# Turning the row maxima with one matmul and one DMA per group, a new order of SyncE's DMAs, maxima 17 units ahead, and six early output tiles

## The chip, the cores and the metric

One of the eight NeuronCores of a Trainium2 chip runs the whole kernel. The metric is device time in microseconds of one execution. Five engines work beside each other, each with its own instruction queue in program order: TensorE (PE) multiplies, VectorE (DVE), ScalarE (ACT) and GpSimd (POOL) compute element by element, and SyncE (SP) only issues DMAs. An instruction that waits for a semaphore holds everything behind it on its own engine. Nearly all DMAs of the first half of this kernel are issued by SP.

## The reference

Causal attention with a multiplicative decay, on 8 batches of 8 heads, 576 tokens and head dimension 64, and after it a mixture of experts, which picks one of 8 experts for each token.

```python
scores = scale * np.matmul(q, k.transpose(0, 1, 3, 2))
cum = np.cumsum(np.log(np.clip(f, 0.0001, 1.0)), axis=-1)
decay = cum[:, :, :, None] - cum[:, :, None, :]
scores = np.where(causal, -1000000000.0, scores + decay)
scores = scores - np.max(scores, axis=-1, keepdims=True)
attn = np.exp(scores); attn = attn / (np.sum(attn, axis=-1, keepdims=True) + 1e-09)
x = np.matmul(attn, v)                       # heads side by side: (8, 576, 512)
# per token: e = argmax(x @ w_gate), or the expert of the token before where a local gate says so
out[b, s] = p[e] * (np.maximum(x[b, s] @ w1[e], 0.0) @ w2[e])
```

## The kernel before

**Attention in 25 units.** Every batch is cut into 25 units of work in five groups. A group 0 to 3 is a pair of heads with five units (`cunit`, `aunit` twice, `bunit`, `cunit`); group 4 has the last 64 queries of all heads, in four `d1unit` and one `d2unit`. A unit has stages, each on one engine: `sc` (PE: scores, transposed, keys on the partitions), `ex` (ACT: exp), `hi` (ACT: the f16 upper part of the result, tile `ph`), `lo` (DVE: the rest, tile `pl`) or, for the units in `SUBS`, `sub` (PE subtracts `ph`) and `lo2` (ACT copies the rest), `av` (PE: three products with the parts of v), and for some `n1` and `n2` (DVE: division by the sum).

**The maxima.** Exp needs the maximum of each query row, which is taken ahead. For each unit there is a maximum: `sm` (PE: leading scores, queries on the partitions, into tile `sm` of the two-bank pool `psM`) and `mx` (DVE: negated row maximum into a column of `nmq`). When the last maximum of a group is there, `sh` follows: DVE transposes `nmq` in blocks of 32 x 32 into `nmt` (line 918), and SP sends it with four DMAs, one per block row, into row 70 of the group's part of `QB` (line 927). Row 70 meets a row of ones in `KB`, so the second matmul of each score block (line 872, `KB` and `QB`, 71 rows) subtracts the maximum. Thus the scores of a group wait for `mx`, the transpose, the place of the four DMAs in SP's queue, and their landing. `LM` (10) says how many units ahead of its own unit a maximum is put into the planner's lines.

**Turned q and k.** The leading scores and the scores need q and k of the next batch turned: SP loads them as f32, POOL splits them into f16 parts (`t16q`, `t16k`), PE transposes eight blocks (`tq`, line 397), ACT or DVE evicts them into `Aq`, `Ak` (`eq`, line 406 to 410; `TE` says which engine), and SP copies the upper part into `QB`, `KB` (line 377, 381). `TS` lists from which unit of the batch before a group's turn may start, `LI` the units at which the loads of the batch after are issued. The maxima of a group need the copies of that group.

**x.** The normalised output `xn` is split by POOL (`xr`, `xl`), turned by a DMA transpose on SP (line 741, 772: `xt`, `xlt`) and written to DRAM (line 747, 779: `xs`) for the experts.

**The planner.** The order of instructions on each engine is made while the program is built. `issue` keeps a line per stage and a `clock` per engine, works out the earliest start of each line's head (`start_of`) from costs written beside each stage, adds a lead per stage (`LEADS`) and emits the stage that is earliest. POOL's work is emitted in portions (`pump`, line 342) with a clock of its own: `clock["POOL"] = max(clock["POOL"], clock["PE"]) + 1.1 * c` (line 348). The planner has no clock for SP: each DMA stands in SP's queue where the code that issues it happens to run, the transposes of x right behind the emission of POOL's split, v's loads with `ship` at given units. For the maxima and the turned copies it counts 3500 ns from the end of the producer to the landing (line 1179).

**The early experts.** While the routing of the last batches is worked out, PE runs the first three tiles of 128 tokens of experts 0 and 1. Their six outputs are evicted by ACT into tiles `o` (line 1763) of which there are three, scaled by POOL (line 1734) when the probabilities are there, and scattered by an indirect DMA (line 1735); a tile is free when its scatter has landed.

Of the kernel before, what the change touches and what calls it, by code (L numbers as in the profile page):

```python
# [34 lines left out]
SUBS = ((2, 4, 10, 13, 14),) * 8  # L35
# [15 lines left out]
LI = (12, 14)  # L51
PX = 5
XI = 2
# [6 lines left out]
RANKS = ((134.0, 26.4, 114.9, 242.4, 23.9, 178.9, 202.3, -22.5, 146.6, -22.2, -144.4, -13.8, 9.1, 28.6, 47.5, 5.3),) * 8  # L60
LEADS = ((-214, -102, -294, -258, -210, -30, -680, -129, -443, -278, -132, -206, -132, -210, -43),) * 8
LM = 10
DMAW = 0.0
# [16 lines left out]
XL = 5300  # L80
# [17 lines left out]
def kernel(  # L98
# [291 lines left out]
    def group(b, nm, j):  # L390
        U = {}

        def tq():
            t16 = Tq[b][nm + "t"]
            U["pt"] = psS.tile([128, 8, 128], F16, name="st")
            for a in range(4 if j == 4 else 8):
                nc.tensor.transpose(U["pt"][:, a], t16[:, 8 * j + a], ident16)

        def eq():
            A, pt = Tq[b][nm + "A"], U["pt"]  # L400
            dst, src = flat(A[:, 8 * j:min(8 * j + 8, 36)]), flat(pt[:, 0:4 if j == 4 else 8])
# [9 lines left out]
            if j < 4:  # L411
                copy_hi(b, nm, 2 * j, 2 * j + 2)
            else:
                copy_last(b, nm)

        c = 0.5 if j == 4 else 1.0
        eng, cost = ("ACT", 130 + 880 * c) if TE[b][nm][j] == "A" else ("DVE", 100 + 570 * c)
        return {"key": (b, nm, j), "tq": ("PE", 460 * c, tq, {"psS": 1}, {}), "eq": (eng, cost, eq, {}, {"psS": 1})}

    def prep_turned(b, nm):  # L420

        def begin():
            add_turns(99)
            if line["eq"]:
                issue((line["eq"][-1][0], "eq"))
            new_prep(b, nm)
            prep_aug(b, nm)

        def half(g0, g1):
            R = {}  # L430

            def parts(i):
                t, t16 = LT[b, nm], Tq[b][nm + "t"]
# [12 lines left out]
    def prep_v(b):  # L446
        i = b % 2

        def part(g0, j):
            return hi_lo(VH[i][:, g0:g0 + 16, 0:64], VL[i][:, g0:g0 + 16, 0:64], LT[b, "v"][:, g0:g0 + 16], 8)[j][1]()  # L450

        def rest(u):
            split(vlast(VH[i], u)[:, :, 0:64], vlast(VL[i], u)[:, :, 0:64], LT[b, "v"][u * 64:(u + 1) * 64, 32:36], False)

        return ([(1024, lambda g0=g0, j=j: part(g0, j)) for g0 in (0, 16) for j in range(3)] +
                [(768, lambda u=u: rest(u)) for u in range(2)])

    def prep(b):

        q, k, v = prep_turned(b, "q"), prep_turned(b, "k"), prep_v(b)  # L460
        done = set()

        def mark(nm):
            return (0, lambda: done.add(nm))

        bulk.extendleft(reversed([(c, lambda: True, lambda c=c: load_v(b, last=c == 4, cs=range(c, min(c + 1, 4))))
                                  for c in range(5)]))
        last = [(5500, init_route)] if b == 2 else []
        if b + 1 < B:
            for nm, i in ("q", LI[0]), ("k", LI[1]):  # L470
                bulk.append((i, lambda nm=nm: nm in done, lambda nm=nm: (new_load(b + 1, nm), load_main(b + 1, nm, 0, 0, H))))
                bulk.append((i + 1, lambda nm=nm: nm in done, lambda nm=nm: load_main(b + 1, nm, 1, 0, H)))
                bulk.append((i + 2, lambda nm=nm: nm in done, lambda nm=nm: load_last(b + 1, nm)))
        return q[:1] + k[:1] + q[1:5] + k[1:5] + q[5:] + [mark("q")] + k[5:] + [mark("k")] + v + last
# [205 lines left out]

    HS = {}
# [10 lines left out]
    def due_head(nm):  # L692
        head_hi(HS[2, nm], 2, nm)
        head_b(HS[2, nm], 2, nm)
        head_lo(HS[2, nm], 2, nm)
        turned[0, nm, -2] = clock["ACT"] + 960 - 3500
        clock["ACT"] += 960
        clock["DVE"] = max(clock["DVE"] + 640, clock["ACT"] + 800)

    def head_3(nm):  # L700
# [6 lines left out]
        def eq():  # L707
            for f in head_hi, head_b, head_lo:
                f(U["st"], 3, nm)
            clock["DVE"] = max(clock["DVE"], clock["ACT"] + 1100) + 640  # L710

        return {"key": (0, nm, -1), "tq": ("PE", 500, tq, {"psS": 1}, {}), "eq": ("ACT", 960, eq, {}, {"psS": 1})}
# [19 lines left out]
    def finish_main(b, xn):  # L732
        xr = pools["small"].tile([128, 4, 2, DM], F16, name="xr", bufs=1)
# [11 lines left out]

        def put_x(r):
# [4 lines left out]
        bulk.extendleft([(0 if b == B - 1 else PX + 2 * r, lambda: 2 in R, lambda r=r: put_x(r)) for r in (1, 0)])  # L751
# [8 lines left out]
        for c in range(0, 4, 2):  # L760
            todo += hi_lo(xr[:, c:c + 2, 0, :], xr[:, c:c + 2, 1, :], xm[:, c:c + 2], 1)
            todo.append((0, lambda c=c: turn_x(c)))
        queue.extendleft(reversed(todo))

    def finish_last(b, xnl):
        xl = pools["small"].tile([128, 2, 4, 64], F16, name="xl", bufs=1)
# [4 lines left out]
        def turn_x():  # L771
# [3 lines left out]
            XR[b] = max(clock["POOL"], clock["PE"]) + XL  # L775
# [10 lines left out]
        else:  # L786
            for i, x in enumerate(hi_lo(xl[:, 0], xl[:, 1], xnl, 4) + [(0, turn_x)]):
                queue.insert(min(XI, len(queue)) + i, x)

# [36 lines left out]
    nmq = cst.tile([128, 2, 5, 32], F16, name="nmq")  # L826
    nmt = cst.tile([128, 2, 5, 32], F16, name="nmt")
    nc.gpsimd.memset(nmq, 0.0)

    def compute(b, T):  # L830
# [69 lines left out]
        def maximum(g, scoref, maxf, cost, takes=1, last=None):  # L900
# [6 lines left out]
            if last:  # L907
                M["sh"], M["key"] = ("DVE", cost[2], last, {}, {}), (b, "shift", g)
# [7 lines left out]
        def turn_shift(g):  # L916

            nc.vector.transpose(nt[:, g], nq[:, g])
            f = flat(QBb[70:71])
            for i in range(4):  # L920
                src = nt[32 * i:32 * i + 8, g]
                if g < 4:
                    dst = f[:, 1024 * g:1024 * g + 1024].rearrange("p (y i x) -> p y i x", i=4, x=32)[:, :, i]
                else:
                    src = src[0:4]
                    dst = f[:, 4096 + 256 * (i // 2):4352 + 256 * (i // 2)].rearrange("p (y i x) -> p y i x", i=2, x=32)[:, :, i % 2]
                nc.sync.dma_start(out=dst, in_=src)
# [56 lines left out]
        def d1unit(j):  # L984
# [14 lines left out]

            def sh():  # L1000
                nc.vector.tensor_tensor(nq[:, 4, 0:4], nm[:, 0:4], nm[:, 4:8], ALU.min)
                turn_shift(4)
# [11 lines left out]
            maximum(4, sm, mx, (680 if j == 0 else 300, 930 if j == 0 else 598, 250), 1 + (j == 0), sh if j == 3 else None)  # L1014
# [72 lines left out]
        def cunit(j, r):  # L1087
# [20 lines left out]
            maximum(j, sm, mx, (275, 598, 160), 1, (lambda: turn_shift(j)) if r == 1 else None)  # L1108
# [42 lines left out]
    STAGES = ("sm", "mx", "mn", "sh", "sc", "ex", "hi", "lo", "sub", "lo2", "av", "n1", "n2", "tq", "eq")  # L1151
# [3 lines left out]
    clock = {"PE": T0, "ACT": T0 + 900, "DVE": T0 + 1300, "POOL": T0}  # L1155
    due = deque()
    pools = {}
# [5 lines left out]
    def start_of(st):  # L1163
# [78 lines left out]
    def issue(until=None):  # L1242
        while any(line.values()):
# [5 lines left out]
            ready = [x for x in ready if x[0] is not None]  # L1249
            if not ready:  # L1250
# [11 lines left out]
            for r, c in takes.items():  # L1262
                for _ in range(c):
                    room[r].remove(min(room[r]))
            fn()
            clock[eng] = t + cost
            ends[n, st] = t + cost, eng
            if st in ("eq", "sh"):
                turned[u["key"]] = t + cost + (0 if st == "eq" else DMAW)
# [468 lines left out]
    def experts(W, xT, nt, prob, scat, hp, op, width=608, every=6, half=None, sums=None):  # L1738
# [276 lines left out]
    issue()  # L2015
    late = early_weights(stage, W0, range(6, 8), shared=7)
    queue.extend(late[:-4])
    pump(0)
    ship(99)
    while chain:  # L2020
# [150 lines left out]
    def close_attention():  # L2171
# [6 lines left out]
        EX["oe"] = ectx.enter_context(tc.tile_pool(name="oe", bufs=3))  # L2178
# [466 lines left out]
```

## Time and profile before

| | us |
|---|---|
| median of 3 runs (lowest, highest) | 915.76 (915.65, 917.53) |
| the profiled execution | 924.86 |
| its span, first to last instruction | 923.1 |
| PE busy in the span | 769.3 (83%) |
| DVE, ACT, POOL busy | 544.4, 476.2, 442.5 |
| attention, about | 31 to 515 |
| experts, about | 515 to 923 |

The profile is of one execution and is a little longer than the median. A busy time is the union of the engine's instructions; a wait is the idle time just ahead of an instruction, put down to what ended it. The granted clock is the share of TensorE's full clock that was granted in a stretch: 1.00 is 2.4 GHz and 0.50 is 1.2 GHz.

### The profile page before, as it was taken

To read this page: it belongs to the slowest core of one execution; us is meant where nothing else is said; L and a number is where in the kernel's file an instruction comes from. 1 tells how busy PE (TensorE), PEld (TensorE's weight loads), DVE (VectorE), ACT (ScalarE), POOL (GpSimd) and SP (SyncE) were. 2 spreads that over 40 slices of the span, in tenths; PEclk is the share of its full clock that TensorE was granted. 3 is DMA by queue.
4 is the path that set the end of the run, shared out by engine and by line. 5 is a ranking of instruction groups with operands and counts; after the bars stand their busy time and mean duration, and the time that the engine had idled before them with its cause. 6 is when DMAs were issued, how large, how long until landed. Compare 5 with 4: busy or idle time off the path is not lost. (4 is left out here: it accounts for less than half of the span.)

```text
span 923.1 us, 24010 instructions
## 1 busy us (share of the span) xinstructions
PE 769.3 (83%) x9730; PEld 579.2 (63%) x9730; DVE 544.4 (59%) x1263; ACT 476.2 (52%) x837; POOL 442.5 (48%) x498
## 2 busy tenths in 40 slices
PE   6639678578685886868956999999999999998996
PEld 3528567568575775857855645656756566657484
DVE  8528446548585695765854477442666766565740
ACT  8529546567575584766843342332545353534441
POOL 5882671835469256693355623233521181247201
PEclk9769868879798897888976999999999999999999
DMA  5633753573747537573277647365653838181501
GB/s 146 153 68 89 163 125 85 125 165 70 152 106 137 147 70 138 133 137 67 55 202 160 188 153 228 90 152 189 136 209 88 236 89 254 56 264 51 109 14 43
DMA packets 192812, 120.96 MB, mean 131 GB/s; under 512 B 131374, under 2 KB 167662, under 8 KB 192658
## 3 DMA queue, kind: packets, MB, share of 16 engines
q1 hardware_dynamic: 186620, 100.28, 45.8%
q0 software_dynamic: 6080, 19.13, 6.6%
q8 instruction: 77, 1.26, 0.6%
q14 instruction: 35, 0.29, 0.1%
HBM read 72.25 MB, written 19.32 MB: 99 GB/s over the span
## 5 line engine op out<-in xcount | busy, mean ns | idle before, releaser
L872 PE MATMUL st<-QB,KB 71*128 71x128 f16 (+2 forms) x960 | 132.5, 229 | 99.2 <-DMA QB<-nmt 98.7
L938 ACT ACTIVATE st<-st 128x512 f32<-128x512 f32 (+1 forms) x200 | 116.3, 582 | 103.4 <-PE st L878 79.6
L872 PEld LDWEIGHTS <-KB 71*128 71x128 f16 (+1 forms) x960 | 94.1, 109 | 108.3 <-issue 60.6
L946 DVE TENSOR_TENSOR pl<-st,ph 128x512 f16<-128x512 f32 (+1 forms) x160 | 105.1, 665 | 66.2 <-ACT ph L942 54.7
L882 DVE TENSOR_REDUCE nmq<-sm 128x1 f16<-128x512 f32 (+3 forms) x224 | 110.8, 531 | 52.2 <-PE sm L878 49.8
L942 ACT CAST ph<-st 128x512 f16<-128x512 f32 (+1 forms) x200 | 115.0, 578 | 46.6 <-PE xp L896 41.0
L872 PE MATMUL st<-Aq,Ak 128*128 128x128 f16 (+2 forms) x960 | 133.8, 229 | 3.9 <-DVE pl L946 3.7
L1779 PE MATMUL z<-xT,wh 128*128 128x384 f16 (+5 forms) x640 | 120.6, 299 | 5.2 <-DVE hl L1756 5.2
L1768 POOL DMA_INDIRECT out_dram<-o,ranki x26 | 36.4, 1400 | 159.1 <-ACT o L1766 79.8
L896 PE MATMUL xp<-VH,pl 128*128 128x65 f16 (+1 forms) x960 | 98.6, 201 | 1.8 <-DVE pl L946 1.7
L1821 PE MATMUL y<-ul,hh 128*128 128x512 f16 x264 | 100.1, 379 | 0.0
L1821 PE MATMUL y<-uh,hl 128*128 128x512 f16 x264 | 100.1, 379 | 0.0
L1821 PE MATMUL y<-uh,hh 128*128 128x512 f16 x264 | 100.1, 379 | 0.0
L896 PE MATMUL xp<-VH,ph 128*128 128x65 f16 (+1 forms) x960 | 99.1, 202 | 0.0
L863 PE MATMUL sm<-KB,QB 70*128 70x256 f16 (+4 forms) x448 | 81.1, 306 | 21.4 <-DMA KB<-Ak 17.6
L896 PE MATMUL xp<-VL,ph 128*128 128x65 f16 (+1 forms) x960 | 98.7, 201 | 0.0
L872 PEld LDWEIGHTS <-Ak 128*128 128x128 f16 (+1 forms) x960 | 93.8, 109 | 7.2 <-issue 3.9
L896 PEld LDWEIGHTS <-ph 128*128 128x128 f16 (+1 forms) x1920 | 90.1, 107 | 7.6 <-issue 3.7
L1821 PEld LDWEIGHTS <-hh 128*128 128x128 f16 x528 | 51.3, 98 | 57.5
L896 PEld LDWEIGHTS <-pl 128*128 128x128 f16 (+1 forms) x960 | 80.1, 107 | 2.2 <-DVE pl L946 2.0
L1779 PEld LDWEIGHTS <-wh 128*128 128x128 f16 x640 | 63.3, 100 | 28.6 <-issue 6.8
L1779 PE MATMUL z<-xT,wl 128*128 128x384 f16 (+5 forms) x320 | 79.8, 299 | 0.0
(450 smaller groups left out, 1747.5 us busy)
## 6 DMA issues: line engine op xcount, KB each, us to landing
stg<-in_moe_w_dram SPq DMA_DIRECT2D x64, 512.0 KB
xs<-xr SPq DMA_DIRECT2D x16, 512.0 KB
ldq<-in_q_dram SPq DMA_DIRECT2D x14, 512.0 KB
ldk<-in_k_dram SPq DMA_DIRECT2D x14, 512.0 KB
ldv<-in_v_dram SPq DMA_DIRECT2D x56, 128.0 KB
QB<-Aq SPq DMA_DIRECT2D x30, 128.0 KB
KB<-Ak SPq DMA_DIRECT2D x30, 128.0 KB
QB<-nmt SPq DMA_DIRECT2D x128, 0.5 KB
```

The lines of the kernel that those rows point to most:

```text
L863: nc.tensor.matmul(st[p0:p0 + m, co:co + n], lhsT=block(QBb, 70, h, c), rhs=rhs, start=(first and co == col), stop=True, skip_group_check= ...
L872: nc.tensor.matmul(st[p0:p0 + m, col:col + n], lhsT=block(tk, kk, h, kc), rhs=block(tq, kk, h, c), start=(ps == 0 and (i == 0 or p0 > 0 an ...
L882: nc.vector.tensor_reduce(dst, src, axis=AX.X, op=ALU.max, negate=True)
L896: nc.tensor.matmul(xo, lhsT=a[:, c0:c0 + m], rhs=w[:, vi, :], start=False, stop=(i == n - 1 and jj == 2), skip_group_check=True)
L938: nc.scalar.activation(U["st"][:, :cols], U["st"][:, :cols], AF.Exp)
L942: nc.scalar.copy(U["ph"][:, :cols], U["st"][:, :cols])
L946: nc.vector.tensor_tensor(U["pl"][:, :cols], U["st"][:, :cols], U["ph"][:, :cols], ALU.subtract)
L1768: nc.gpsimd.indirect_dma_start(out=outf, out_offset=bass.IndirectOffsetOnAxis(ap=scat(t)[0:m], axis=0), in_=o[0:m], in_offset=None, bounds ...
L1779: nc.tensor.matmul(z[:, a, 0:wd], lhsT=w[:, d, fc * 128:(fc + 1) * 128], rhs=xT[:, x, a * wd:(a + 1) * wd], start=(i == 0), stop=(i == len ...
L1821: nc.tensor.matmul(y[0:m], lhsT=a[:, fc, t * 128:t * 128 + m], rhs=u[:, fc], start=(i == 0), stop=(i == len(prods) - 1))
```

## The change

- `nmq` shrinks to 8 columns per group and `nmt` becomes 8 rows of 128. Instead of `sh` on DVE there are two stages: `sh` on PE, a matmul of `nmq` (as weights, 8 or 4 columns) with the identity into the bank of the group's last maximum, and `se`, a copy out of PSUM (DVE by `SE`). That bank is freed by `se`, not by `mx`. One DMA sends 8 x 128 values; group 4 has two. The minimum of group 4 (line 1001) moves into `mx`.
- A DMA may be posted with the time at which the planner thinks its producer ends and a cost on SP. `deliver` emits the earliest one and moves a new `clock["SP"]`; `issue` delivers a posted DMA before it emits any stage that starts later. Posted are the sends of maxima, the copies into `QB` and `KB`, the decay rows, the loads of q, k and v, the transposes and writes of x. A consumer calls `need`, so that a tile's load is emitted before POOL's work on it.
- What counts as landed is `clock["SP"] + LAND` (2000 ns), not the producer's end plus 3500 ns.
- `LM` is 17; the parameters of the planner (`RANKS`, `LEADS`, `SW`, `TS`, `TE`, `LI`, `PX`, `XI`) are other ones; `SUBS` has six units instead of five.
- The early experts have six tiles `o`.

```diff
-SUBS = ((2, 4, 10, 13, 14),) * 8
+SUBS = ((1, 7, 12, 20, 21, 24),) * 8
-LI = (12, 14)
-PX = 5
-XI = 2
+LI = (11, 9)
+PX = 6172
+XI = 9
-SW = ((-271, 0, 0),) * 8
-TS = ({'q': (4, 15, 19, 21, 24), 'k': (10, 13, 20, 24, 24)},) * 8
-TE = ({'q': 'AAAAA', 'k': 'DAAAA'},) * 8
+SW = ((-969, 0, 0),) * 8
+TS = ({'q': (4, 16, 18, 21, 19), 'k': (10, 15, 17, 21, 22)},) * 8
+TE = ({'q': 'AADDA', 'k': 'AAAAA'},) * 8
...
-LM = 10
-DMAW = 0.0
+LM = 17
+LAND = 2000.0
+SE = ('DVE', 160)
...
+    def post(ready, cost, fn, tag=None):
+        heapq.heappush(mail, (ready, sent[0], cost, fn, tag))
+        sent[0] += 1
+        if "run" not in EX:
+            deliver()
+
+    def deliver():
+        ready, _, cost, fn, _ = heapq.heappop(mail)
+        clock["SP"] = max(clock["SP"], ready) + cost
+        fn()
+
+    def need(tag):
+        while any(x[4] == tag for x in mail):
+            deliver()
...
+        def posted_x(c):
+            post(clock["POOL"], 2600, lambda: turn_x(c), ("x", b))
+            for r in range(2 if c else 0):
+                post(clock["POOL"] + PX * (r + 1), 630, lambda r=r: put_x(r), ("x", b))
...
-    nmq = cst.tile([128, 2, 5, 32], F16, name="nmq")
-    nmt = cst.tile([128, 2, 5, 32], F16, name="nmt")
-    nc.gpsimd.memset(nmq, 0.0)
+    nmq = cst.tile([128, 2, 5, 8], F16, name="nmq")
+    nmt = cst.tile([8, 2, 5, 128], F16, name="nmt")
...
-                M["sh"], M["key"] = ("DVE", cost[2], last, {}, {}), (b, "shift", g)
+                M["mx"] = "DVE", cost[1], maxf, {}, {"psM": takes - 1}
+                M["sh"] = "PE", 80, lambda: turn_shift(g, last()), {}, {}
+                M["se"] = SE[0], SE[1], lambda: put_shift(g, last()), {}, {"psM": 1}
...
-        def turn_shift(g):
-
-            nc.vector.transpose(nt[:, g], nq[:, g])
+        def turn_shift(g, st):
+
+            m = 8 if g < 4 else 4
+            nc.tensor.matmul(st[0:m, 0:128], lhsT=nq[:, g, 0:m], rhs=ident16, start=True, stop=True, skip_group_check=True)
+
+        def put_shift(g, st):
+            m = 8 if g < 4 else 4
...
+                nc.vector.tensor_copy(nt[0:m, g], st[0:m, 0:128])
             f = flat(QBb[70:71])
-            for i in range(4):
-                src = nt[32 * i:32 * i + 8, g]
...
-                nc.sync.dma_start(out=dst, in_=src)
+
+            def send():
+                if g < 4:
+                    nc.sync.dma_start(out=f[:, 1024 * g:1024 * g + 1024], in_=nt[0:8, g])
...
+                turned[b, "shift", g] = clock["SP"] + LAND
+
+            post(clock[SE[0]], 600 if g < 4 else 1200, send)
...
-                after.append((turned[key] + 3500, "POOL"))
+                after.append((turned[key], "POOL"))
...
+            if mail and mail[0][0] <= min((x[0] for x in ready), default=1e9):
+                deliver()
+                continue
...
-            o = (EX["oe"] if op is ep else op).tile([128, DM], F32, name="o", bufs=3)
+            o = (EX["oe"] if op is ep else op).tile([128, DM], F32, name="o", bufs=6 if op is ep else 3)
```

## Rows read from the trace of the kernel before

**Rows 1.** The page's 40 slices: TensorE's granted clock, in tenths.
```profile
PEclk9769868879798897888976999999999999999999
```

**Rows 2.** Windows: stretch, length, busy PE, PEld, DVE, ACT, POOL; clock, DMA.
```profile
63.00:124.40 61.40, 46.33 (x819) 40.53 (x820) 32.82 (x75) 37.48 (x64) 35.91 (x39) 0.81 0.52 110
...
sum 411.90, PE 316.05 PEld 279.77 DVE 262.90 ACT 263.02 POOL 226.80; mean PE 45.15 PEld 39.97 DVE 37.56 ACT 37.57 POOL 32.40
```

**Rows 3.** Windows between the long waits, the same seven batches.
```profile
302.90:350.30 47.40, 43.91 (x881) 39.10 (x881) 39.46 (x102) 36.28 (x66) 21.29 (x26) 0.95 0.50 116
...
sum 347.90, PE 314.40 PEld 279.19 DVE 242.67 ACT 255.55 POOL 180.54; mean PE 44.91 PEld 39.88 DVE 34.67 ACT 36.51 POOL 25.79
```

**Rows 4.** Waits of PE, 20 to 520 us: total, times, longest.
```profile
PE st L872 <- DMA QB<-nmt: 98.7, 18, 15.9
PE sm L863 <- DMA KB<-Ak: 17.6, 5, 4.9
```

**Rows 5.** Timeline of DVE near 287 us: start, length, instruction.
```profile
286.69 0.21 DVE L918 STREAM_TRANSPOSE nmt<-nmq 128x32 f16<-128x32 f16 x1
```

**Rows 6.** Timeline of SP's queue, 282 to 305 us.
```profile
283.96 1.57 SPq L741 DMA_TRANSPOSE xt<-xr  x1
285.64 1.92 SPq L772 DMA_TRANSPOSE xlt<-xl  x1
...
288.95 1.82 SPq L741 DMA_TRANSPOSE xt<-xr  x1
...
294.44 4.36 SPq L203 DMA_DIRECT2D ldv<-in_v_dram  x2
298.90 2.82 SPq L927 DMA_DIRECT2D QB<-nmt  x4
```

**Rows 7.** Timeline of PE; in brackets the idle time before and what ended it.
```profile
31.61 0.27 PE L872 MATMUL st<-QB,KB 71*128 71x128 f16 x1 [6.02 <-DMA QB<-nmt]
...
302.88 0.27 PE L872 MATMUL st<-QB,KB 71*128 71x128 f16 x1 [11.37 <-DMA QB<-nmt]
302.94 0.31 PE L872 MATMUL st<-Aq,Ak 128*128 128x128 f16 x1
```

**Rows 8.** Windows behind nine of the waits; columns as in rows 2.
```profile
302.90:307.80 4.90, 4.90 (x65) 4.90 (x66) 2.37 (x6) 2.15 (x4) 1.92 (x2) 0.50 0.77 169
...
sum 47.80, PE 47.75 PEld 43.13 DVE 13.67 ACT 21.47 POOL 22.81; mean PE 5.31 PEld 4.79 DVE 1.52 ACT 2.39 POOL 2.53
```

**Rows 9.** Groups by shape, 20:520 us: count, busy us, mean ns, idle.
```profile
L949 PE MATMUL st<-ph,minus 128*128 128x512 f16 x40 | 17.0, 425 | 0.8 <-ACT ph L942 0.7
...
L946 DVE TENSOR_TENSOR pl<-st,ph 128x512 f16<-128x512 f32 x152 | 101.8, 679 | 65.4 <-ACT ph L942 54.1 <-PE xp L896 7.9 <-PE st L949 3.1
...
L918 DVE STREAM_TRANSPOSE nmt<-nmq 128x32 f16<-128x32 f16 x40 | 8.4, 209 | 1.0
...
L819 DVE TENSOR_TENSOR L<-st,half 128x36 f32<-128x36 f32 x7 | 1.3, 190 | 0.1
...
L406 ACT ACTIVATE Aq<-st 128x1024 f16<-128x1024 f16 x30 | 30.7, 1026 | 17.0 <-PE st L397 16.9
...
L954 ACT CAST pl<-st 128x512 f16<-128x512 f32 x40 | 23.4, 588 | 11.2 <-PE st L949 11.0
```

**Rows 10.** Waits of ACT from 515 us on: total, times, longest.
```profile
ACT o L1763 <- DMA out_dram<-o,xs: 14.9, 3, 6.8
```

**Rows 11.** Timeline of PE at the early experts.
```profile
586.62 0.27 PE L1779 MATMUL z<-xT,wh 128*128 128x256 f16 x1 [2.17 <-DVE hl L1756]
```

**Rows 12.** The window behind it; columns as in rows 2.
```profile
586.70:592.00 5.30, 5.30 (x35) 4.11 (x35) 1.65 (x9) 0.77 (x2) 2.72 (x4) 0.68 0.26 99
```

**Rows 13.** Two dense windows of 20 us; columns as in rows 2.
```profile
420.00:440.00 20.00, 19.94 (x389) 17.68 (x387) 13.31 (x38) 15.59 (x29) 8.56 (x10) 0.90 0.30 67
...
380.00:400.00 20.00, 20.00 (x413) 18.35 (x412) 15.18 (x35) 14.70 (x25) 14.89 (x21) 0.84 0.42 98
```

**Rows 14.** Waits of POOL, 60 to 515 us: total, times, longest.
```profile
POOL xr L335 <- DVE xn L976: 55.3, 5, 21.1
```

More of the change, by code (lines that the diff above doesn't have):

```diff
@@ L410, in eq, with copy @@
                 nc.vector.tensor_copy(dst, src)
[L411 to L414, printed above, removed]
+            def copy():
+                if j < 4:
+                    copy_hi(b, nm, 2 * j, 2 * j + 2)
+                else:
+                    copy_last(b, nm)
+                turned[b, nm, j] = clock["SP"] + LAND
+            post(clock["ACT" if TE[b][nm][j] == "A" else "DVE"], 550, copy)
         c = 0.5 if j == 4 else 1.0
@@ L426, in begin @@
             new_prep(b, nm)
-            prep_aug(b, nm)
+            post(clock["SP"], 750, lambda: prep_aug(b, nm), ("aug", b))
         def half(g0, g1):
@@ L464, in mark, with load @@
             return (0, lambda: done.add(nm))
-        bulk.extendleft(reversed([(c, lambda: True, lambda c=c: load_v(b, last=c == 4, cs=range(c, min(c + 1, 4))))
+        def load(nm, cost, fn):
+            post(clock["POOL"], cost, fn, ("ld", nm))
+        bulk.extendleft(reversed([(c, lambda: True,
+                                   lambda c=c: load("v", 1300, lambda: load_v(b, last=c == 4, cs=range(c, min(c + 1, 4)))))
                                   for c in range(5)]))
@@ L695, in due_head @@
         head_lo(HS[2, nm], 2, nm)
-        turned[0, nm, -2] = clock["ACT"] + 960 - 3500
+        turned[0, nm, -2] = clock["ACT"] + 960
         clock["ACT"] += 960
@@ L709, in eq @@
                 f(U["st"], 3, nm)
-            clock["DVE"] = max(clock["DVE"], clock["ACT"] + 1100) + 640
-        return {"key": (0, nm, -1), "tq": ("PE", 500, tq, {"psS": 1}, {}), "eq": ("ACT", 960, eq, {}, {"psS": 1})}
+            clock["DVE"] = max(clock["DVE"], clock["ACT"] + 140) + 640
+        return {"own": True, "key": (0, nm, -1), "tq": ("PE", 500, tq, {"psS": 1}, {}), "eq": ("ACT", 960, eq, {}, {"psS": 1})}
     def first_turns():
@@ L750, in finish_main @@
         R = {}
-        bulk.extendleft([(0 if b == B - 1 else PX + 2 * r, lambda: 2 in R, lambda r=r: put_x(r)) for r in (1, 0)])
+        if b == B - 1:
+            bulk.extendleft([(0, lambda: 2 in R, lambda r=r: put_x(r)) for r in (1, 0)])
         if b == B - 1:
@@ L774, in turn_x @@
             XD[b] = XD.get(b, 0) + 1
-            XR[b] = max(clock["POOL"], clock["PE"]) + XL
+            XR[b] = clock["SP"] + LAND
         def put_xl():
@@ L786, in finish_last @@
         else:
-            for i, x in enumerate(hi_lo(xl[:, 0], xl[:, 1], xnl, 4) + [(0, turn_x)]):
+            for i, x in enumerate(hi_lo(xl[:, 0], xl[:, 1], xnl, 4) +
+                                  [(0, lambda: post(clock["POOL"], 2600, turn_x, ("xl", b)))]):
                 queue.insert(min(XI, len(queue)) + i, x)
@@ L1154 @@
     now = [0]
-    clock = {"PE": T0, "ACT": T0 + 900, "DVE": T0 + 1300, "POOL": T0}
+    clock = {"PE": T0, "ACT": T0 + 900, "DVE": T0 + 1300, "POOL": T0, "SP": T0}
     due = deque()
+    mail = []
+    sent = [0]
     pools = {}
@@ L1264, in issue @@
                     room[r].remove(min(room[r]))
+            clock[eng] = t + cost
             fn()
-            clock[eng] = t + cost
             ends[n, st] = t + cost, eng
-            if st in ("eq", "sh"):
-                turned[u["key"]] = t + cost + (0 if st == "eq" else DMAW)
+            if u.get("own") and st == "eq":
+                turned[u["key"]] = t + cost
             for r, c in frees.items():
@@ L2015 @@
     issue()
+    while mail:
+        deliver()
     late = early_weights(stage, W0, range(6, 8), shared=7)
@@ L2019 @@
     ship(99)
+    while mail:
+        deliver()
     while chain:
@@ L2177, in close_attention @@
         stage2 = EX["stage"] = ctx.enter_context(tc.tile_pool(name="stage2", bufs=ST))
-        EX["oe"] = ectx.enter_context(tc.tile_pool(name="oe", bufs=3))
+        EX["oe"] = ectx.enter_context(tc.tile_pool(name="oe", bufs=6))
         first = early_weights(stage2, EX["W"], range(NP), 1)
```

41 lines of the change are left out of this document (24 added, 17 removed).

## The prediction, made before the changed kernel was run

> **What bounds the kernel now.** I read the page first: its slices and the line PEclk show two halves. From about 515 us to the end TensorE (PE) is busy nearly without a break and its clock is granted in full; before that, in attention, the granted clock falls again and again [rows 1]. So the change, which touches attention and one detail behind it, is judged in attention. There I cut the trace at the third group of each batch, where PE always waits: seven batches of 25 units take 411.9 us, 58.8 us each, and in a batch PE is busy 45.2, VectorE (DVE) 37.6, ScalarE (ACT) 37.6 and GpSimd (POOL) 32.4 us [rows 2]. No engine fills the batch; something makes them wait. Cut instead from the end of one such wait to the start of the next, the same 25 units take 347.9 us, 49.7 each, and the best of them 47.4 [rows 3]. The waits of PE name the cause: 98.7 us in 18 waits, up to 15.9, for the DMA that puts the negated maxima into row 70 of QB; the next, for copies of turned keys, is 17.6 us in 5 [rows 4].
>
> Why that DMA is late is seen in one example. DVE turned the maxima at 286.69 us [rows 5]. SyncE (SP) issued their four DMAs at 298.90, because in its queue stood transposes of x that waited for POOL, writes of x, and two loads of v that alone held SP for 4.36 us [rows 6]. PE resumed at 302.88, after 11.37 us of idling [rows 7]. The last of the four was taken up at about 301.0 (298.90 and three quarters of 2.82), 1.9 us before. So the transfer is short; its place in the queue is the cost.
>
> **The change part by part.** The sum is made against the profiled execution, 924.86 us, span 923.1. It stands 1.0% above the median of the three plain runs, 915.76, so the result is multiplied by 0.990.
>
> *17 units ahead, and SP's order.* Maxima move 7 units further ahead. A unit takes 49.7/25 = 1.99 us between waits, so the DMA gets up to 13.9 us more; with one DMA where there were four, another 2.1 us (three quarters of 2.82 [rows 6]). The new order puts the send where the planner's clocks end its producer, and x's transposes and v's loads likewise, so that less stands ahead of it. The long waits are 411.9 - 347.9 = 64.0 us in seven, and 15.9 in the first batch, 79.9 together: all are shorter than 16.0 us. I take 75 of these as gone, and half of the other 18.8 (the very first group has no earlier units to go ahead of: its 6.02 us [rows 7] lose the 2.1), 9: **-84**. Bounds: -98.7, and -60 if lead alone helps and SP is held as before.
>
> *The clock behind the waits.* After nine of the waits PE is busy throughout but gets 0.50 to 0.58 of its clock, the 1.2 GHz level, for 47.8 us in all, 4.9 after the example [rows 8]. At 2.4 GHz that work takes half: at most -23.9. ACT and DVE would then set the pace for some of it; **-12**, half.
>
> *What comes late next.* The maxima, put earlier, read keys and queries that have to be turned and copied earlier: POOL's split, PE's turn, ACT's copy, a DMA on SP. The list of turns for groups 1 to 4 moves by less than 7 units (group 2, q and k, from units 19 and 20 of the batch before to 18 and 17, while its maxima go from unit 25, the batch's own start, to 18), so the slack there goes. PE's queue is in order: a maximum that waits holds the scores, the products with v and the turns behind it, and ACT and DVE run dry. Today such a wait costs 17.6/5 = 3.5 us [rows 4]. Four groups in seven batches are exposed, 28; I take 6 new waits, **+21**. Bounds 0 and 28 x 3.5 = 98.
>
> *Small instructions.* Forty turns by matmul: nothing like an 8-column product with the identity stands in the trace; next to each other 128-column products start 0.06 us apart [rows 7], and the widest evidence is 0.43 us for a 512-column one [rows 9]; 0.06 is the nearer form, 2.4 us. Forty copies out of PSUM replace forty DVE transposes of 209 ns [rows 9]; the nearest read of a few columns from PSUM takes 190 ns, so nothing (bounds -8 and +8). Eight more units cut by PE instead of DVE: 8 x 0.43 = 3.4 us of PE against a DVE pass of 0.68 each [rows 9]. Turns change engine (two of q to DVE, one of k to ACT): per batch ACT loses 1.03 and gains 0.59 for the added sixth cut, and DVE stays about level; both are far from full, so nothing, and if one of them were to set the pace, half a microsecond a batch. Two of the PE terms overlap idle time: **+3** in all, bounds -5 and +14. The new hop from DVE to PE and back (about as long as a transpose) lies inside the lead; without that cover it would cost about two transposes, 0.4 us a group. The bank it holds longer is one of two for maxima, once in five.
>
> The Trainium skill (VectorE: DVE Perf Modes, "The three transpose paths" and the rules behind it) speaks against this part: DVE's own transpose of a 32 x 32 block is called the fastest, 311 ns for a 128 x 128 tile against 390 on TensorE plus a copy. By its figures and a copy of 190 ns each group would lose 0.27 us, an estimate, and the sum would be -65 if none of it were covered, against -76. The trace agrees that the transpose is cheap (209 ns here), and shows besides it the four DMAs that its block layout forces, which the page does not count.
>
> *Six early output tiles.* ACT waits 14.9 us in three waits for scatters of o [rows 10]. On PE this is one gap of 2.17 us [rows 11] and then 5.3 us at 0.68 of the clock [rows 12], 1.7 us lost: **-4**; bounds 0 and -14.9.
>
> Sum: -84 - 12 + 21 + 3 - 4 = **-76**, 848.9 us in a profiled execution, 841 plain. A cross-check by density: the fullest stretch of ACT that I see without a long wait keeps it busy 15.59 of 20 us, 78% [rows 13]; 37.1 us of ACT per batch at that share is 47.6 us, 11.2 less than today, 78 over seven batches, and 16 of the first: -98 with the output tiles, 819 plain. The sum is weighed heavier, since it has the new waits in it: I predict **840 us**.
>
> **The rivals.**
>
> *SP is still held.* The order is right only as far as POOL's clock is. Line 348 lets POOL start with PE and counts its work, but POOL really waits for DVE's normalised output, 55.3 us in 5 waits, up to 21.1 [rows 14]; the send behind such a transpose waits with it. Against: 13.9 us of lead are under all but the worst. If each batch keeps 21.1 - 13.9 = 7 us, 56 of the 98.7 us stay; the waits give 43 less, the clock 5: 924.9 - 43 - 5 + 3 - 4 = 876, 867 plain.
>
> *The clock stays low.* For it: in 380 to 400 us PE is busy all 20.0 us and yet has 0.84 of its clock [rows 13], with no long wait near. If short waits take the place of long ones, the 12 us don't come, and PE keeps paying: -84 + 21 + 3 - 4 = -64, 861, 852 plain. The Trainium skill (TensorE: Matmul & The Clock Gate, "A second HAM failure mode: psum-queue depth-cycling") describes this: short idling between groups of matmuls is enough to make the clock swing between its levels. By that rule 852 holds; the 0.84 of the trace agrees with it.
>
> *The turned copies decide: slower.* One mechanism: the maxima of groups 1 to 4, now first in PE's order, wait for KB and QB. Today's worst such wait is 4.9 us [rows 4]. If all 28 take that, +137 against -84 - 12 + 3 - 4 = -97: 965, 955 plain. It is slower from 97/28 = 3.5 us a group on, just what such a wait costs now. Against: only 5 of them wait today, the planner schedules a maximum only after its estimate of the copy, and the loads of q and k move earlier too (units 11 and 9, from 12 and 14).
>
> **How the numbers follow.** Forecast (gain of 60 to 125 us in the profile, the upper end being all of 98.7 and of 23.9, the tiles' 4, less 2 for the matmuls) 0.60, SP held 0.17, clock 0.15, turned copies 0.08. The forecast's own range is thus 792 to 856. To leave out no more than 2 in 10 I take 800 to 885: it takes in the clock and the held queue, and leaves out the slower case and the very best one. Repeated runs of this kernel differ by about 0.2%, so that is the line for no change. Faster by more: nearly all of the first three, 0.90; slower: 0.07 of the fourth; no change 0.03.
>
> **What would show it.** Right: PE's waits for the DMA from nmt fall from 98.7 to under 20 us; the send follows the copy on SP within 2 or 3 us; a batch takes 46 to 51 us; the granted clock in attention rises from about 0.85 to over 0.9; PE's waits for KB rise to 25 to 45 us; no gap at the early output tiles. Wrong: sends 10 us behind their producers, or waits for KB and QB of over 90 us, or ACT or DVE over 85% busy in batches that still take 55.

## The result, and the profile after

The changed kernel takes **848.47 us** (median of 4 runs, 844.62 to 855.01), the kernel before took 916.64 (4 runs on the same chip, 915.65 to 921.08). The ratio is **0.9255, 95% interval 0.9187 to 0.9322**: 7.5% faster. By that ratio the 915.76 us of the heading become 847.5; 840 was forecast.

The profiled execution took 844.62 us (span 842.9) against 924.86 (923.1): 80.2 us less, 12 more than the medians say, since the one is the fastest of its four runs and the other lies above the range of its own. Where these 80.2 us lie, cut at the third group of each batch as before and at the first expert's first matmul (all in us):

| stretch | before | after | difference |
|---|---|---|---|
| start to the first cut | 63.0 | 59.6 | -3.4 |
| seven batches | 411.9 | 345.2 | **-66.7** |
| last cut to the first expert ("the join") | 39.8 | 39.4 | -0.4 |
| experts | 408.4 | 398.7 | -9.7 |

The clock that TensorE (PE) was granted, in 40 slices of the page of after, against [rows 1]:

```profile
PEclk9879897989998998999978999999999999999999
```

In attention, the first 21 slices, three digits lie below 8; of the first 22 before, eight did. The windows of the seven batches of after (stretch, length, busy PE, PEld, DVE, ACT, POOL, clock, DMA share, GB/s) answer to [rows 2]:

```profile
59.60:108.40 48.80, 45.36 (x812) 38.78 (x812) 36.31 (x79) 34.59 (x61) 23.59 (x29) 0.88 0.50 111
...
211.70:258.80 47.10, 42.56 (x867) 36.27 (x865) 42.78 (x97) 36.89 (x68) 39.50 (x48) 1.00 0.73 158
...
sum 345.20, PE 306.82 PEld 266.72 DVE 268.93 ACT 254.50 POOL 231.13; mean PE 43.83 PEld 38.10 DVE 38.42 ACT 36.36 POOL 33.02
```

A batch takes 49.3 us where it took 58.8. The sums split the 66.7: PE's busy time falls by 9.2 us (316.05 to 306.82, while the clock of the stretch rises from 0.84 to 0.93), its idle time by 57.5 (95.85 to 38.38). One batch now runs at the full clock throughout. The waits of PE, 20 to 520 us, in after (total, times, longest) answer to [rows 4]:

```profile
PE sm L899 <- DMA QB<-Aq: 17.2, 6, 5.7
PE st L908 <- DMA QB<-nmt: 13.3, 2, 12.0
PE sm L899 <- DMA KB<-Ak: 12.5, 5, 4.3
PE z L1831 <- DMA xT<-xg: 11.5, 1, 11.5
```

The waits for the maxima are gone but for one of 12.0 us. The copies of turned queries and keys are now waited for 29.7 us (0.8 and 17.6 before), and the first expert waits 11.5 us for its tokens, which it did not. How a send now stands on SP, from the timeline of SP's queue in after, against [rows 6]; VectorE (DVE) ended the two copies of maxima ahead of these sends at 289.68 and 297.63:

```profile
289.71 0.70 SPq L969 DMA_DIRECT2D QB<-nmt  x1
290.51 0.48 SPq L378 DMA_DIRECT2D QB<-Aq  x1
291.08 0.55 SPq L378 DMA_DIRECT2D KB<-Ak  x1
...
294.77 1.84 SPq L770 DMA_TRANSPOSE xt<-xr  x1
297.66 0.73 SPq L969 DMA_DIRECT2D QB<-nmt  x1
298.50 1.71 SPq L770 DMA_TRANSPOSE xt<-xr  x1
300.30 7.19 SPq L204 DMA_DIRECT2D ldv<-in_v_dram  x8
307.59 0.70 SPq L969 DMA_DIRECT2D QB<-nmt  x1
```

Both are issued 0.03 us behind their producers; the eight loads of v, 7.19 us of SP, stand behind. The third send shows what is left of the old trouble: its producer ended at 304.0, and it stood 3.6 us behind those loads. What the turn costs, by shape, 20 to 520 us of after (count, busy us, mean ns, idle before), against [rows 9]:

```profile
L997 PE MATMUL st<-ph,minus 128*128 128x512 f16 x40 | 16.2, 405 | 0.4 <-ACT ph L990 0.4
L964 DVE CAST nmt<-sm 8x128 f16<-8x128 f32 x32 | 8.7, 273 | 8.6 <-PE sm L957 8.4
L957 PE MATMUL sm<-ident,nmq 128*8 128x128 f16 x32 | 7.1, 222 | 0.9 <-DVE nmq L918 0.9
```

Two groups of SP's DMAs, 63 to 400 us, the first of before, the second of after (instruction, count: shortest, median and longest ns, first and last start):

```profile
L927 SPq DMA_DIRECT2D QB<-nmt x115: 572/635/2187, 62.7 to 397.6; - x115
```

```profile
L969 SPq DMA_DIRECT2D QB<-nmt x28: 652/712/2221, 63.4 to 392.6; - x28
L971 SPq DMA_DIRECT2D QB<-nmt x14: 572/648/1491, 72.0 to 369.6; - x14
```

L927 sends 512 bytes (256 in group 4), L969 2 KB, L971 512 bytes. A DMA of 512 bytes holds SP's queue nearly as long as one of 2 KB, 0.64 us against 0.71 in the median, and longer than a copy of turned keys of 128 KB, 0.54 us in the kernel before:

```profile
L377 SPq DMA_DIRECT2D KB<-Ak x24: 461/541/1285, 75.9 to 394.5; - x24
```

So among plain DMAs it is their number that fills this queue, hardly their bytes. In that stretch SP's queue was taken up for 242.5 us by 330 DMAs before and for 231.6 by 289 after (summed from its records), 42 and 34 us per batch. The queue is not full, then; what counts is what stands ahead of a DMA that is waited for.

### The profile page after: what moved, and what is told of

Its sections match the earlier page's. It is cut to its first block, busy times and chain, and to the rows that moved or that the text cites. A ratio compares the mean times of both kernels' runs of the same rounds, so it can differ in the third digit from the quotient of the medians.

```text
span 842.9 us, 23982 instructions
## 1 busy us (share of the span) xinstructions
PE 752.8 (89%) x9778; PEld 559.9 (66%) x9778; DVE 556.4 (66%) x1264; ACT 468.6 (56%) x836; POOL 436.5 (52%) x497
## 5 line engine op out<-in xcount | busy, mean ns | idle before, releaser
L986 ACT ACTIVATE st<-st 128x512 f32<-128x512 f32 (+1 forms) x200 | 115.6, 583 | 43.3 <-PE st L914 19.4
L908 PE MATMUL st<-QB,KB 71*128 71x128 f16 (+2 forms) x960 | 120.6, 217 | 13.3 <-DMA QB<-nmt 13.3
L1831 PE MATMUL z<-xT,wh 128*128 128x384 f16 (+5 forms) x640 | 118.9, 296 | 12.2 <-DMA xT<-xg 11.5
L908 PE MATMUL st<-Aq,Ak 128*128 128x128 f16 (+2 forms) x960 | 120.8, 217 | 2.0 <-DVE pl L994 1.7
L994 DVE TENSOR_TENSOR pl<-st,ph 128x512 f16<-128x512 f32 x152 | 102.1, 678 | 12.7 <-ACT ph L990 12.1
L1820 POOL DMA_INDIRECT out_dram<-o,ranki x26 | 28.0, 1078 | 157.3 <-ACT o L1818 86.6
L899 PE MATMUL sm<-KB,QB 70*128 70x256 f16 (+4 forms) x448 | 79.7, 298 | 32.7 <-DMA QB<-Aq 17.2
L908 PEld LDWEIGHTS <-Ak 128*128 128x128 f16 (+1 forms) x960 | 86.9, 102 | 21.2 <-issue 17.8
L932 PE MATMUL xp<-VH,pl 128*128 128x65 f16 (+1 forms) x960 | 91.8, 195 | 2.5 <-DVE pl L994 2.5
L932 PE MATMUL xp<-VH,ph 128*128 128x65 f16 (+1 forms) x960 | 92.7, 197 | 0.0
L932 PE MATMUL xp<-VL,ph 128*128 128x65 f16 (+1 forms) x960 | 92.1, 195 | 0.0
L908 PEld LDWEIGHTS <-KB 71*128 71x128 f16 (+1 forms) x960 | 87.4, 102 | 4.3 <-issue 2.8
L932 PEld LDWEIGHTS <-ph 128*128 128x128 f16 (+1 forms) x1920 | 83.0, 103 | 7.8 <-issue 2.6
L1831 PEld LDWEIGHTS <-wh 128*128 128x128 f16 x640 | 62.4, 98 | 35.2 <-issue 14.3
```

The costliest lines, as they stand in the source:

```text
L899: nc.tensor.matmul(st[p0:p0 + m, co:co + n], lhsT=block(QBb, 70, h, c), rhs=rhs, start=(first and co == col), stop=True, skip_group_check= ...
L908: nc.tensor.matmul(st[p0:p0 + m, col:col + n], lhsT=block(tk, kk, h, kc), rhs=block(tq, kk, h, c), start=(ps == 0 and (i == 0 or p0 > 0 an ...
L932: nc.tensor.matmul(xo, lhsT=a[:, c0:c0 + m], rhs=w[:, vi, :], start=False, stop=(i == n - 1 and jj == 2), skip_group_check=True)
L986: nc.scalar.activation(U["st"][:, :cols], U["st"][:, :cols], AF.Exp)
L994: nc.vector.tensor_tensor(U["pl"][:, :cols], U["st"][:, :cols], U["ph"][:, :cols], ALU.subtract)
L1820: nc.gpsimd.indirect_dma_start(out=outf, out_offset=bass.IndirectOffsetOnAxis(ap=scat(t)[0:m], axis=0), in_=o[0:m], in_offset=None, bounds ...
```

## The experiments

The theory at the start was the prediction's: lead and order took the waits away, and the count of DMAs is a detail. Its rival, the theory after the first four runs, is that SP's queue itself is what is short: it is helped twice, by fewer DMAs in it and by sends that stand where their producers end, while the lead by itself and the planner's settings by themselves do nothing. Each ratio is to runs of the kernel before on the same chip. The runs stand on several chips, on which the median of the kernel before lies between 916.64 and 926.97 us; single profiles that are set side by side below can differ by a per cent from this alone.

**Four DMAs with everything else of the change.**

```
- nc.tensor.matmul(st[0:m, 0:128], lhsT=nq[:, g, 0:m], rhs=ident16, ...)
+ nc.vector.transpose(nt[:, g], nq[:, g])
+ for i in range(4): ... nc.sync.dma_start(out=dst, in_=src)
+ post(clock["DVE"], 2800, send)
```

> The changed kernel with the old turn: a DVE transpose of 32 by 32 blocks and four DMAs per group, in the new order, 17 units ahead. Theory: 2 us more of SP per group lie inside the lead, so 847 to 856 us and at most 10 us more of waits. Rival D (fewer DMAs carry the gain): 865 us and more.

Measured 897.05 us, **0.9707** (0.9657 to 0.9757). By the ratio that is 889.8 on the scale of 916.64, some 34 us above the first theory's range: four DMAs do not simply lie inside the lead. The rival holds. Its seven batches, DVE's transpose and four DMAs that the planner counts as 2.8 us:

```profile
63.40:433.20 369.80, 314.89 (x5963) 276.11 (x5964) 264.18 (x638) 253.77 (x460) 224.66 (x273) 0.89 0.61 126
```

Of the 54.9 us by which this profile is longer than after's, 24.6 lie in the batches, 16.4 in the join (55.8 us), 10.1 in the experts and 3.8 in the start.

**One DMA, the code's order; and 10 units ahead.** The first delivers each DMA where the code stands; the second changes `LM`.

```
- if "run" not in EX:
-     deliver()
+ deliver()
```

> The changed kernel, but every DMA is issued where the code that makes it stands, not in the order of the planner's ends (17 units ahead and the one-DMA turn stay). Theory (place in SP's queue is the cost; lead and order each cover a part): sends of the third groups stand 7 to 14 us behind their producers again, the lead of 10 to 14 us covers most of it; PE waits 15 to 35 us for the DMA of the maxima, 858 to 880 us. Rival L (lead alone does it): waits stay under 15 us, 845 to 853 us. Rival O (order alone does it): waits of 60 us and more, 895 to 910 us.

> The changed kernel with maxima 10 units ahead instead of 17. Theory: 4 to 6 us from the turned maxima to the scores, against a send that stands 0 to 6 us and lands about 2 us later: PE waits 15 to 35 us for this DMA, its waits for QB and KB go down by about 10, 858 to 875 us. Rival L: the long waits return, 890 to 915 us. Rival O: 846 to 854 us.

873.5 us, **0.9444** (0.9409 to 0.9479), and 869.22, **0.9396** (0.9362 to 0.9429). The first is in its range: the order, on top of the rest, is worth 1.9% of the time before. The second is in its range too (861.3 by the ratio), but not for the reason expected: it is slower than after, and not in its batches, which are if anything shorter. Its window over them, cut at the same place:

```profile
59.70:398.50 338.80, 303.66 (x6009) 266.22 (x6009) 271.50 (x643) 254.96 (x463) 226.80 (x274) 0.94 0.65 136
```

The loss is in the join, 66.5 us against 39.4. SP's queue of the same kernel shows it:

```profile
440.64 11.70 SPq L1769 DMA_TRANSPOSE xT<-xg  x6
452.44 1.34 SPq L971 DMA_DIRECT2D QB<-nmt  x2
```

The last group's maxima were copied at 435.1, too late to get ahead of the transposes of the first experts' tokens; PE waited 19.5 us. So the 17 units are worth nothing in the steady state, and with them go 27 us in the join of these two profiles (1.4% of the time, 13 us, by the medians). That the lead itself saves the join is not shown: a kernel below with 17 units loses the join in the same way, and the one DMA alone, with 10 units, has the shortest join of all.

**17 units ahead alone.** The kernel before with one number changed.

```
- LM = 10
+ LM = 17
```

> The kernel before with maxima 17 units ahead and nothing else. Theory: the lead takes off about half of the waits (98.7 us to 35 to 60), since SP is held as before; 865 to 890 us. Rival L: 850 to 862 us. Rivals O and D: 905 to 917 us.

923.67 us, **0.9992** (0.995 to 1.0035), no change, far above the 865 to 890 of the theory; its PE waits, 20 to 520 us:

```profile
PE st L872 <- DMA QB<-nmt: 108.1, 17, 16.8
PE sm L863 <- DMA KB<-Ak: 20.2, 7, 5.9
```

The rank in the planner's list moves, the instruction does not, most likely because the maxima still have to wait for turned keys and queries, whose units did not move: the time from the turned maxima to their group's first score, for the third group of batches 2 to 7, stays 5.9 us (6.0 before).

**What the planner is told of the four DMAs.** In the first experiment it reckoned 2.8 us of SP's time for a send; here it is told 0.6 (1.2 for group 4) for four DMAs, and 2.8 for the one.

```
- post(clock["DVE"], 2800, send)
+ post(clock["DVE"], 600 if g < 4 else 1200, send)
```

> The changed kernel with the DVE transpose and four DMAs per group, but the planner counts them on SP like the one DMA (600 ns, 1200 in group 4) instead of 2800. Theory S (the four DMAs really hold SP, 2 us a group, 84 us of its queue): the loss of the four-DMA version stays, 0.96 to 0.975 of the time of the kernel before. Theory P (the loss came from the planner, which put other work off because it took SP for fuller): 0.925 to 0.94.

> The changed kernel, whose one DMA per group is counted by the planner as 2800 ns of SP, though it takes 0.7. Theory S: nothing really holds SP longer, 0.925 to 0.935 of the time before. Theory P: 0.955 to 0.975.

Four DMAs told as cheap: 913.88, **0.9948** (0.99 to 0.9996), above both ranges. One told as dear: 859.98, **0.9357** (0.9289 to 0.9425), a hair above theory S's range. Neither theory covers this alone. What SP really does counts: told the same 2.8 us, the four DMAs (0.9707) are 3.5% behind the one. But what is reckoned counts too: told too little, four DMAs lose another 2.4%, and their seven batches take 382.0 us where they took 369.8; told too much, one DMA loses 1.0% (the intervals overlap), though its batches are as short as any:

```profile
59.80:400.30 340.50, 304.97 (x5997) 263.83 (x5997) 266.54 (x637) 253.57 (x461) 227.48 (x275) 0.94 0.66 140
```

It loses in the join, 61.4 us, as the kernel with 10 units did: the last maxima, copied by 429.66, stood on SP behind the six transposes of the first experts' tokens, with 17 units of lead, and PE waited 22.3 us for them.

```profile
434.68 12.45 SPq L1769 DMA_TRANSPOSE xT<-xg  x6
447.23 1.57 SPq L770 DMA_TRANSPOSE xt<-xr  x1
448.90 1.90 SPq L971 DMA_DIRECT2D QB<-nmt  x2
```

PE's waits with four cheap DMAs:

```profile
PE st L909 <- DMA QB<-nmt: 33.8, 8, 17.6
PE sm L900 <- DMA KB<-Ak: 28.6, 7, 8.2
PE sm L900 <- DMA QB<-Aq: 25.0, 9, 6.3
PE z L1824 <- DMA xT<-xg: 15.2, 1, 15.2
```

The copies of turned q and k, which are through SP 1.6 to 1.7 us behind the end of their producers in after, are through 3.9 to 4.0 us behind here (means of 38 each).

**The planner's settings alone; three output tiles.** The first is the kernel before with after's cut units, turn units and engines, ranks, leads, loads and `LM` (`PX` and `XI`, which it reads in another way, stay); the second is after with `bufs=3` for the early tiles.

> The kernel before with the planner's parameters of the changed one (17 ahead, ranks, leads, turn units, load units, units cut by PE), but with the old turn, four DMAs and SP's order as the code stands. Theory (the queue is the cost, and the parameters help only with its new order): 0.97 to 1.01, PE waits 60 us and more for the DMA of the maxima. Rival Q (other parameters carry the gain): 0.95 and less.

> The changed kernel with three early output tiles instead of six. By the prediction's term 4 us are lost: 0.927 to 0.932 of the time before, a gap of about 2 us on PE at the early experts again. Rival (the tiles carry the whole 9.7 us by which the experts' part became shorter): 0.934 to 0.938.

917.42, **0.997** (0.9929 to 1.001): nothing by themselves. 851.32, **0.9259** (0.9173 to 0.9346), just under the 0.927 of its theory: the six tiles are not to be seen beside 0.9255. ScalarE (ACT) waits for the scatters again in the second, and PE does not care:

```profile
ACT o L1815 <- DMA out_dram<-o,xs: 14.6, 3, 7.0
```

This kernel does the same work as after up to the experts, and its seven batches took 351.6 us at a clock of 0.91 against 345.2 at 0.93: that is how far apart two single profiles of one program lie.

**The count of DMAs by itself.** The matmul's turn stays, its eight rows leave in four DMAs of two rows.

```
- nc.sync.dma_start(out=f[:, 1024 * g:1024 * g + 1024], in_=nt[0:8, g])
+ for i in range(4):
+     c = 1024 * g + 256 * i
+     nc.sync.dma_start(out=f[:, c:c + 256], in_=nt[2 * i:2 * i + 2, g])
```

> The changed kernel, still turned by the matmul and evicted by VectorE into eight rows, but the eight rows leave in four DMAs of two rows each instead of one (group 4: four of two rows instead of two of four). Nothing else differs, and the planner is told the same queue times. Theory (the number of DMAs on SP's queue is what counts, whatever form the maxima have): some 60 more DMAs between 63 and 400 us, SP 0.65 us each, so the copies of q and k come late again as in the kernel with four DMAs from the DVE transpose (0.9948 of the kernel before): 0.97 to 0.995, waits for the maxima and for the copies together over 60 us. Rival (the block form and the DVE transpose themselves held things up): as the changed kernel, 0.925 to 0.94, waits under 45 us.

892.76, **0.9615** (0.9577 to 0.9654): between the two ranges, and by its waits (73 us for maxima and copies) the theory's. Its seven batches are as long as those with DVE's transpose and four DMAs (379.2 and 382.0 us): in the batches the form of the turn costs nothing that can be seen, the count does. What parts the two profiles most is the join, 42.4 against 58.7.

**One DMA alone**, in the kernel before with its own settings and order.

```
+ M["mn"] = "PE", 80, lambda: turn_shift(g, last()), {}, {}
+ M["sh"] = "DVE", 160, lambda: put_shift(g, last()), {}, {"psM": 1}
```

> The kernel before with the matmul turn and one DMA alone: its own settings of the planner, maxima 10 units ahead, DMAs where the code stands, three output tiles. Theory (the DMA count alone carries most): 0.945 to 0.97, with waits for the maxima's DMA falling from 98.7 us to 30 to 60. Rival (the count pays only with the reordered sends): 0.985 to 1.0, waits for the maxima still 80 us or more, since the copy of the maxima still stands behind the copies of q and k on SP.

887.1, **0.9584** (0.9539 to 0.9629), in its range; the waits for the maxima fell to 67.5 us, less far than the 30 to 60 expected.

```profile
61.90:450.10 388.20, 314.20 (x6063) 271.40 (x6063) 272.20 (x671) 262.25 (x464) 240.88 (x288) 0.89 0.62 134
```

A batch takes 55.5 us here, 3.4 less than before, 23.7 in all; another 12.5 of its gain is the join, 27.3 us for 39.8.

The windows over the seven batches of four kernels with the same settings make a table of two by two. The settings alone (four DMAs, code's order):

```profile
63.60:479.40 415.80, 326.95 (x6029) 286.03 (x6030) 277.83 (x665) 258.08 (x464) 233.73 (x281) 0.85 0.55 121
```

Four DMAs, ordered, told as 0.6 us (DVE's transpose, then the split send; the first experiment, told as 2.8, has 369.80):

```profile
65.00:447.00 382.00, 311.38 (x5985) 273.48 (x5986) 266.61 (x638) 253.30 (x460) 221.80 (x270) 0.90 0.57 124
```

```profile
62.00:441.20 379.20, 315.79 (x5996) 274.08 (x5996) 267.42 (x642) 255.18 (x461) 229.46 (x277) 0.89 0.56 124
```

One DMA, code's order:

```profile
59.90:432.70 372.80, 326.19 (x6073) 280.48 (x6073) 280.29 (x662) 257.71 (x464) 232.97 (x279) 0.89 0.62 132
```

Per batch (a seventh): 59.4 with neither; 53.3 with one DMA; 52.8, 54.2 or 54.6 with the order; 49.3 with both, which is after. One DMA gives 6.1 us without the order and 3.5 to 5.3 with it (4.2 if both are told as 2.8 us), the order 4.8 to 6.6 and 4.0: about the same, and they roughly add up. Only two of the steps are single edits, from the split send to after (4.9) and from the code's order to after (4.0): the kernel with neither also lacks the other changes, such as the new reckoning of the landing. And two profiles of one program differ by 0.9 a batch.

Put on in this order, they work differently. PE's idle time (length less busy PE) falls from 88.9 us to 46.6 by the one DMA; by the order, on top of that, it falls by only 8.2 more, and 19.4 us come from busy PE, whose clock goes from 0.89 to 0.93; three times what two profiles of one program lay apart. The other way round it is not so: the order first takes 18 to 34 us from PE's idle time and 11 to 16 from busy PE.

**Two attempts to go further.** The first puts the first batch's late send ahead of the loads that delayed it; the second, besides, puts the last batch's splits of x behind the gathers for the first experts.

```
- ('b', 29000)
+ ('b', 31500)
```

> The changed kernel with the last set-up step of the first batch due at 31.5 us of the planner's time instead of 29, so that the DMA of the first batch's third group stands on SP ahead of that step's loads. Theory: the 12.0 us wait of the first batch goes and 6 to 10 us with it, 0.914 to 0.920. Rival: what was loaded early now comes late, the copies of the second batch's q and k wait instead, 0.924 to 0.932.

> The same as the one before it, and in the last batch the splits of the normalised rows and their transposes are put behind the gathers of the first experts' tokens on POOL and behind their transposes on SP. Theory: the wait of 11.5 us for the first expert's tokens shrinks by 3 to 6 us, so 0.909 to 0.917 (3 to 6 us under the kernel with the earlier send alone). Rival: the rows of the last batch are then written late and the experts that need them wait: no gain, 0.915 to 0.93.

867.16, **0.9365** (0.9327 to 0.9402), and 868.51, **0.9377** (0.9342 to 0.9412): both slower than after, by more than the rivals had it. The first send gained its 3.9 us (first cut at 55.7), then seven batches took 355.4 us with no more idling than after (38.9 against 38.4) but at a clock of 0.90, and the join took 52.3. There POOL's timeline shows why:

```profile
441.65 2.36 POOL L340 TENSOR_TENSOR ul<-stg,uh 128x512 f16<-128x512 f32 x2
...
453.38 1.12 POOL L1764 DMA_INDIRECT xg<-xs,xg  x1 [0.17 <-issue]
```

The indices for the gathers were ready at 439.52, yet the gathers stood behind splits of the weights until 453.38: after the shift the planner no longer reached them before its list of units ended, and what is left over is issued behind the weights. The second attempt met the same (gathers from 448.94), so its own idea was not tested.

## Why the prediction was right, and where not

The direction, the kernel's limit and the size held: -80.2 us in the profile against -76 (68 us by the medians). That the sum came so near is in part luck, since the largest term is right for wrong reasons and the misses of the others cancel. Term by term, from one profile to the other:

- *Waits for the maxima's DMA, -84:* 98.7 to 13.3, **-85.4**. Right in sum, wrong in its two reasons. Seven units further ahead were credited with 13.9 us of lead; alone they gave nothing, and in after the 10.9 us of lead at the third group (6.0 before) come for the most part from the other settings, turns and loads among them: with 10 units it is still 8.5. With these settings but the old sends the lead is 14.0, and the waiting is only shared out: 46.0 us for maxima, 41.1 for keys. One DMA for four was credited with 2.1 us more of lead a group, its own delay. It is worth 3.4 to 6.1 us of time a batch, 4.9 where nothing else differs. The 14 DMAs that a batch has fewer, some 0.64 us of SP each, had stood ahead of *everything* in the queue: from the split send to after the copies of q and k start 1.1 us behind their producers instead of 2.2 and 2.9, the sends 1.5 instead of 2.5 (means), and PE's waits for both fall from 73 to 43 us.
- *The first batch's 15.9, counted as gone:* 12.0 stay. The set-up of the first batch is issued as the code stands, and its third send, ready at 43.6, was issued at 57.8 behind loads of v and the decay rows:

```profile
52.96 2.63 SPq L204 DMA_DIRECT2D ldv<-in_v_dram  x4
55.86 1.82 SPq L207 DMA_DIRECT2D ldv<-in_v_dram  x2
57.78 0.72 SPq L969 DMA_DIRECT2D QB<-nmt  x1
```

- *Clock, -12:* busy PE in the seven batches, with the added small matmuls in it, **-9.2**.
- *Copies late next, +21:* 18.4 to 29.7, **+11.3**. The queries, not the keys: the waits for KB, forecast to rise to 25 to 45 us, fell from 17.6 to 12.5, those for QB rose from 0.8 to 17.2; 11 waits of 2.7 us. In the three kernels with four DMAs and the order it is 33 to 54 us.
- *Small instructions, +3:* 40 turns at 222 ns are 8.8 us where 2.4 were taken, but they overlap their neighbours (one starts at 296.80 and the next product at 296.95), so PE's share lies between; and the copies take 273 ns where DVE's transpose took 209; no run parts this from the clock.
- *Output tiles, -4:* **not to be seen**; the row of waits of ACT was no proof that PE felt it. The experts' -9.7 is then mostly no effect of the change: with three tiles they took 400.6, and in other kernels with the experts of before 401.0 and 403.8.
- *Not foreseen, +11.5:* the first expert's wait for its tokens. The last batch ends its scores 12.5 us sooner after its cut (22.8 us for 35.3) and gives 12.1 of them back. In the new order the routing comes later: the indices for POOL's gathers are ready 24.6 us after the cut (9.8 before), and the first gather starts 27.7 us after it (10.1), behind splits of x:

```profile
485.03 1.13 POOL L1712 DMA_INDIRECT xg<-xs,xg  x1 [1.18 <-DVE xs L1634]
```

```profile
432.45 1.12 POOL L1764 DMA_INDIRECT xg<-xs,xg  x1 [0.17 <-issue]
```

  The first line is of before (cut at 474.90), the second of after (404.80).

With the experts' -9.7 these add up to -81.5; the rest is small waits, and PE's busy time in the start and the join.

Of the rivals, "SP is still held" was the nearest to life: the kernels that lack the one DMA or the order land at 873 to 914 us, above its 867, and keep part of the waits. It did not come: the sends start 1.5 us behind the end of their producers on average and are through SP 2.4 us behind (4.6 and 7.6 before). "The clock stays low" came in part where the order was undone (busy PE 326.19). "Turned copies decide" was seen with four DMAs told as cheap, 53.6 us, which is 35.2 more than before and a quarter of its 137, and even there the kernel was not slower than before.

The Trainium skill (DMA: Bandwidth & Descriptors, "Issuing engines are not separate DMA queues") says that the time a sequencer takes to start a DMA is usually small beside the DMA itself. For one send that is borne out only loosely: the first batch's late one held SP 0.72 us, and PE went on at 59.60, 1.82 us after its start. Summed over a queue it misleads: a send of 512 bytes holds SP's queue for 635 ns, and 160 of them against 48 were about half of the gain in the batches, while the 16 DMA engines were busy for 0.55 of the time in the kernel before. Of the transposes the Trainium skill (VectorE: DVE Perf Modes, "The three transpose paths") says that DVE's is the faster. The trace agrees, 209 ns against 222 on PE and 273 for the copy out of PSUM, and the runs show that it decides nothing here: with four DMAs each, both turns give batches of 53 to 55 us.

What stays open: why the planner's order, with one DMA, works mostly through the granted clock; and how much of the differences of one or two per cent between kernels is the planner's luck, since each edit gives another order of everything, as the shift of one due time by 2.5 us showed (1.1% slower). No run with settings fitted to four DMAs was made, so their price holds for settings that were made for one. And some 12 us of the join are open: the one DMA alone ended its join in 27.3 us, and no run shows after's batches with such a join.

## What to carry to other kernels

Count the instructions of an in-order queue, not their bytes: if tiny DMAs share a queue with copies on the critical path, each one is paid by all that stands behind it, and a layout that needs one DMA where there were four can be worth a slower way to make it. A wait that is taken away shows up at the next thing in that queue; look there before crediting the lead. And cut a pipelined kernel into steady state and end: three kernels whose seven batches lie within 7 us of each other (345.2, 338.8, 340.5) had joins of 39.4, 66.5 and 61.4.

## What the runs showed that was not expected

A DMA of 512 bytes and one of 2 KB take SP's queue 635 and 712 ns in the median, and some over 2 us; one of 128 KB takes 541. With the same instructions (after, and after with three output tiles) the granted clock of seven batches was 0.93 and 0.91, 6.4 us apart. With as little idling of PE as after (38.9 and 38.4 us in seven batches), the earlier first send had a clock of 0.90 and 9.7 us more of busy PE.
